# Three edits in an attention and MLP kernel: where the first loads are issued, which banks the first transposes use, and the order of the first layer's products

## The chip, the cores and the metric

The kernel runs on one core of one Trainium2 chip. A core has TensorE (PE, matmuls and transposes, results in PSUM banks), VectorE (DVE), ScalarE (ACT, table functions and copies), GpSimd (POOL) and SyncE (SP, which here only issues transfers). Each engine works through its own list of instructions in order and waits on semaphores for the others. Transfers between memory and the core run on 16 DMA engines; SP and ACT issue them to hardware queues (q1 is SP's, q10 ACT's in the profile), POOL to a software queue (q0).

The metric is device time in microseconds: the median of several runs. Before the change it is 442.35 us, from three runs between 442.12 and 442.97.

## What is computed

Eight batches of 12 heads, 448 positions, head size 64; then a two-layer MLP over the 3,584 rows:

```python
def rmsnorm(x, g):
    rms = np.sqrt(np.mean(x * x, axis=-1, keepdims=True) + 1e-06)
    return x / rms * g
q_n, k_n = (rmsnorm(q, g_q), rmsnorm(k, g_k))
scores = scale * np.matmul(q_n, k_n.transpose(0, 1, 3, 2))
scores = scores - np.max(scores, axis=-1, keepdims=True)
attn = np.exp(scores)
attn = attn / (np.sum(attn, axis=-1, keepdims=True) + 1e-09)
x = np.matmul(attn, v)                      # heads side by side: 3584 x 768
h = x @ w_in                                # 768 x 2048
g = gelu_tanh(h)
return g @ w_out                            # 2048 x 768
```

## The kernel before, in words

**Tiling.** A batch's positions stand on 112 partitions, four positions to each. Heads go in pairs (six pairs, `hp`), and in three chunks of four heads (two pairs) for loading. A pair fills 128 partitions once transposed. The first layer's 2,048 columns go in 16 blocks of 128 (`f`), over six steps of 128 inputs, one per pair (`c`); step `c` needs only that pair's x.

**A batch's way.** For each chunk q and k are loaded (`load`, L95), squared (L120 on ACT, L122 on POOL), summed over the head size (DVE, L127), turned into 1/rms by a logarithm and an exponential (ACT, L136 `lg` and L139 `rinv`), and multiplied (`nrmq`, `nrmk`, L149, on DVE or POOL). A pair is then transposed by PE (`trans`, L166, four transposes for q and four for k into the PSUM tile `tp`) and copied out, q to `qT` (L172 on ACT for the first pair, L174 on DVE for others), k to `kT` (L175, DVE) times `gcol`, the product of the two gain rows g_q and g_k. Scores (PE, L204) go through the exponential (ACT, L208). Sums and products with V (PE, L234) end in three DVE steps, `st`, `rc`, `rb` (L244 to L246), and in `xT` (L251).

**Order.** The schedule is written out by hand: each engine's order is the order of the calls. The first batch has an attention of its own (`first_attention`, L397), since nothing else is there to fill PE. Here `idle` (L144) multiplies zeros to keep PE at work. POOL squares and norms most of the first batch, and issues V's loads (L111), both halves of `win` (L483) and of `wout` (L489) between. `gpsimd_waits` (L529, `mark`) is a copy of one element that holds POOL until the second pair's `nrmk` is there.

**The start.** Before the first square, SP's list holds the first chunk's loads in halves of two heads (q, k, q, k), then the second chunk's the same way (q, k, q, k), then whole chunks. ACT's list begins with the loads of g_q and g_k (L68) and a table load (L437). POOL's begins with a memset of `ident`, a memset of `kT` (L84) and a select that finishes `ident`; its next instruction squares the second chunk's first half of q, and its next issues V's first two heads. A transfer takes one of eight hardware semaphores in turn (software transfers have their own), and the ninth waits until the first has landed. On DVE the order is: sums, `gcol` (L499), `gdiag` (L501), the first pair's `nrmq` and `nrmk`, three steps of `shift`, `kT`. PE multiplies by `gdiag` (L503, for `shift`), runs three fill products, the first pair's eight transposes, three more fill products, and the first scores. `ps_m` is a pool of two PSUM tiles that take turns.

**The end of the first batch's attention.** `first_attention` ends with the last pair's sums and products, and with two calls of `mm1_pair` (L331): each fills two blocks `f`, 12 products, into one PSUM tile `hh` of two banks, and has ACT take both through the gelu (L344). The main program then has DVE sum the next batch's squares, ACT load the exponential's table (L580), compute `lg` and `rinv`, load the gelu's table again (L581), and goes on with pairs 2 to 7.

Of the kernel before, what the change touches and what calls it, by code (L numbers as in the profile page):

```python
# [9 lines left out]
BF16 = mybir.dt.bfloat16  # L10
# [6 lines left out]
def kernel(  # L17
# [11 lines left out]
    nc = tc.nc  # L29
    B, H, S, D = q.shape  # L30
# [34 lines left out]
    nc.vector.memset(zeros, 0.0)  # L65
    grow = consts.tile([D, 2], F32)
    for i, row in enumerate((g_q, g_k)):
        nc.scalar.dma_start(grow[:, i:i + 1], row.rearrange("(d o) -> d o", o=1))  # L68
    EXP_SET, GELU_SET = "natural_log_exp_and_others", "gelu_apprx_tanh_and_others"

    gcol = consts.tile([128, 1], F32)
# [17 lines left out]
    def load(b, c, n, parts=1, eng=nc.sync):  # L89
        t = rawqk.tile([P, CH, NK, D], F32, tag=f"raw{n}", name=f"raw{n}")  # L90
        src = {"q": q, "k": k}[n]
        raws[n, b, c] = t
        m = CH // parts
        return [
            lambda i=i: eng.dma_start(  # L95
                t[:, i * m:(i + 1) * m],
                src[b, c * CH + i * m:c * CH + (i + 1) * m].rearrange(
                    "h (p t) d -> p h t d", t=NK
                ),
            )  # L100
            for i in range(parts)
        ]
# [49 lines left out]
            rinvs[b][:, c, "qk".index(n), 2 * j:2 * j + 2].to_broadcast([P, 2, NK, D]),  # L152
        )

    def trans(b, hp, home=None):

        c, j = hp // (CH // 2), hp % (CH // 2)
        if hp == 0:
            qT[b] = qkp.tile([128, HP, S], BF16, tag="qT", name="qT")
        if home is ps_m:  # L160
            tp = ps_m.tile([128, 2, 512], BF16, tag="mm", name="tp")
        else:
            tp = ps_s.tile([128, 2, 1024], BF16, tag="sc", name="tp")
        for i, n in enumerate("qk"):
            for t in range(NK):
                nc.tensor.transpose(  # L166
                    tp[:, i, t * P:(t + 1) * P],
                    nrms[n, b, c][:, j, t].rearrange("p a d -> p (a d)"),
                    ident[:P, :P],
                )  # L170
        if b == 0 and hp == 0:
            nc.scalar.copy(qT[b][:, hp], tp[:, 0, :S])  # L172
        else:
            nc.vector.tensor_copy(qT[b][:, hp], tp[:, 0, :S])  # L174
        nc.vector.tensor_scalar(  # L175
            kT[:, hp, :, :P], tp[:, 1, :S].rearrange("p (t s) -> p t s", s=P), gcol[:, 0:1],
            None, op0=ALU.mult,
        )

# [151 lines left out]
    def mm1_pair(i, cs=range(HP)):  # L331

        if cs[0] == 0:
            hs1[i] = ps_s.tile([128, 2, 512], F32, tag="sc", name="hh")
        h = hs1[i]
        for j in range(2):
            f = 2 * i + j
            for c in cs:
                nc.tensor.matmul(  # L339
                    h[:, j, :S], win[:, c, f * 128:(f + 1) * 128], xT[0][:, c],  # L340
                    start=(c == 0), stop=(c == HP - 1),
                )
        if cs[-1] == HP - 1:
            nc.scalar.activation(  # L344
                g[:, 2 * i:2 * i + 2, :S], h[:, :, :S], AF.Gelu_apprx_tanh
            )
# [50 lines left out]
    def first_attention(side, mid, early, late):  # L397


        warm = {}  # L400
        for i in range(HP * 2):
            for fn in side.get(i, ()):
                fn()
            scores(0, i // 2, 2 * (i % 2))
            for fn in mid.get(i, ()):
                fn()
            scores(0, i // 2, 2 * (i % 2) + 1)
            if i < 2:
                warm[i] = ps_o.tile([128, S], F32, tag=f"o{i}", name=f"o{i}")
                idle((6, 2)[i], warm[i])  # L410
            for fn in early.get(i, ()):
                fn()
            if i == 1:
                idle(4, warm[i])
            if i >= 2:
                pair_sums(0, i // 2 - 1, i % 2, waits=i < 6)
            for fn in late.get(i, ()):
                fn()
        nc.scalar.preload_act_table_set(GELU_SET)
        square(1, 2, "k", nc.scalar)  # L420
        for what in range(2):
            pair_sums(0, HP - 1, what)
        for i in range(2):
            mm1_pair(i)

    def plan(*entries):
        steps = {}
# [2 lines left out]
        return steps  # L430


    qh, kh = load(0, 0, "q", 2), load(0, 0, "k", 2)
    for i in range(2):
        qh[i]()
        kh[i]()
# [76 lines left out]
        shift, shift, -(D ** 0.5) * (1 + 2.0 ** -8), 60.0, op0=ALU.mult, op1=ALU.add  # L513
    )
    nc.vector.tensor_scalar(shift, shift, 0.0, None, op0=ALU.min)
    trans(0, 0, ps_m)
    idle(3, ps_m.tile([128, 512], F32, tag="mm", name="w")[:, :S])
    square(0, 0, "k", nc.scalar, slice(2, 4))
    totals0(1)
# [28 lines left out]
            (11, lambda: square(1, 1, "k", nc.gpsimd), lambda: square(1, 2, "q", nc.gpsimd),  # L548
             lambda: w_out_part(0), lambda: load_v(1, 0, CH), lambda: w_out_part(1))]
    mid = [(0, lambda: rsqrt0(1))] + [(2 * hp - 3, lambda hp=hp: rsqrt0(hp)) for hp in range(3, HP)]  # L550
    early = [(2 * hp + 1, lambda hp=hp: trans(0, hp + 1, ps_m)) for hp in range(HP - 1)]
    late = [(9, lambda: total(1, 0, "q"))]
    first_attention(plan(*side), plan(*mid), plan(*early), plan(*late))
    def normed1(c):
        for j in range(CH // 2):
            for n in "qk":
                normed(1, c, n, j, nc.vector)

    def transposed(b, c):
        for n in "qk":  # L560
            dma_trans(b, c, n)
# [12 lines left out]
    for b in range(B):  # L574
        m1, side = [], []
        if b == 0:

            m1 = [(1, lambda: total(1, 0, "k"), lambda: total(1, 1, "q"),
                   lambda: total(1, 1, "k"), lambda: total(1, 2, "k"), lambda: total(1, 2, "q"),
                   lambda: nc.scalar.preload_act_table_set(EXP_SET), lambda: rsqrt(1),  # L580
                   lambda: nc.scalar.preload_act_table_set(GELU_SET),  # L581
                   lambda: load_v(1, CH, 2 * CH), lambda: normed1(0), lambda: normed1(1)),
                  (3, lambda: loads(2, 0)),
                  (4, lambda: trans(1, 0, ps_m), lambda: normed1(2), lambda: transposed(1, 1),
                   lambda: loads(2, 1)),
                  (5, lambda: trans(1, 1, ps_m), lambda: loads(2, 2),
                   lambda: pool_waits(1, 2, "k", 1), lambda: square(2, 0, "q", nc.gpsimd),
                   lambda: square(2, 0, "k", nc.gpsimd)),
                  (6, lambda: trans(1, 4, ps_m)), (7, lambda: trans(1, 5, ps_m))]
            side += [(0, lambda: total(2, 0, "q"), lambda: total(2, 0, "k")),  # L590
                     (2, lambda: gain(1, 1))]

            for c, slots in ((1, (5, 7)), (2, (9, 10))):
                for n, slot in zip("qk", slots):
                    side += [(2 * c - 1, lambda c=c, n=n: square(2, c, n, nc.gpsimd)),
                             (slot, lambda c=c, n=n: total(2, c, n))]
        elif b + 1 < B:
            if b > 1:

                m1.append((0, lambda: gpsimd_waits(ess[b, HP - 1][:1, 0, 0, :1])))  # L600
            for c in range(NCH):
                m1 += [(0, lambda c=c: normed_all(b + 1, c)),
                       (4 * c + 4, lambda c=c: transposed(b + 1, c))]
            m1 += [(9, lambda: gain(b + 1, 0)), (14, lambda: gain(b + 1, 1))]
            side.append((3, lambda: gain(b + 1, 2)))
        if 0 < b and b + 2 < B:
            m1 += [(4, lambda: loads(b + 2, 1)), (8, lambda: loads(b + 2, 2))]
            for c, at in ((0, 1), (1, 9)):
                for i, (n, half) in enumerate((n, half) for n in "qk" for half in range(2)):
                    m1.append((at + i, lambda c=c, n=n, half=half: squared(b + 2, c, n, half)))  # L610
                m1 += [(at + 2, lambda c=c: total(b + 2, c, "q")),
                       (at + 4, lambda c=c: total(b + 2, c, "k"))]
            for n in "qk":
                m1.append((13, lambda n=n: square(b + 2, 2, n, nc.gpsimd)))
                side.append((0, lambda n=n: total(b + 2, 2, n)))
        m1 = plan(*m1)
        for f in range(nf // 2 if b == 0 else nf):
            if b > 0:
                mm1(b, f)
            elif f > 1:  # L620
                mm1_pair(f)
            for fn in m1.get(f, ()):
                fn()
        m2 += m2_parts(b)
        if b + 1 == B:
            for fn in m2:
                fn()
            break
        nc.scalar.preload_act_table_set(EXP_SET)
        if b + 2 < B:  # L630
            side += [(11, lambda: rsqrt(b + 2)),
                     (0 if b else 2, lambda: load_v(b + 2, 0, H))]
            if b + 3 < B:
                side.append((1, lambda: loads(b + 3, 0)))
        attention(b + 1, m2, 96 if b == 0 else 112, plan(*side))
# [30 lines left out]
```

## Time and profile before

| What | us |
|---|---|
| median of three runs | 442.35 |
| the profiled execution, its time | 442.38 |
| its span, first to last instruction | 440.6 |
| PE busy | 428.7 |
| ACT busy | 306.2 |
| first exponential (L208) starts | 9.78 |
| first product with V (L234) starts | 18.48 |
| first product of the first layer (L339) starts | 37.08 |
| from here PE has work without a gap worth naming | 47.86 |

An engine's busy time is no bound by itself: PE's 428.7 us hold fill products too. In the chain of waits a step starts when the step before it released it. The rows of the timeline give start, length, engine, line and operation, and in brackets how long the engine stood idle before and for whom.

### The profile page before, as it was taken

The page shows a single profiled execution, that of the slowest core. Times are in us where ns is not written, and L with a number is a line of the kernel's source. Part 1 is how long each engine was busy: PE and PEld are TensorE (multiplying, and loading weights), DVE is VectorE, ACT ScalarE, POOL GpSimd, SP SyncE. Part 2 cuts the span into 40 slices and gives each one's busy share as a digit, 9 for nine tenths or more (in the row PEclk, how much of TensorE's full clock was granted, in tenths as well). Part 3 has the DMA queues.
Part 4 walks back from the last instruction along what each step waited for, and adds up shares of the span by engine and source line. Part 5 has one row for each costly group of instructions (what it writes and reads, how often), then busy time and mean ns, then how long its engine had stood idle before and what let it go on. Part 6 is the DMA issues. An engine that isn't in the chain of part 4 may idle for free.

```text
span 440.6 us, 7132 instructions
## 1 busy us (share of the span) xinstructions
PE 428.7 (97%) x2827; PEld 215.2 (49%) x2827; DVE 258.9 (59%) x446; ACT 306.2 (69%) x407; POOL 149.9 (34%) x138
## 2 busy tenths in 40 slices
PE   8898999999999999999999999999999999999996
PEld 3344554455445554455445544455544554455563
DVE  5889846834688357763688536872588603881010
ACT  5896568946886688857888578856889348863310
POOL 5998126482202940065400950037400730000000
PEclk9999999999999999999999999999999999999999
DMA  8999999569801868139911779119831431111022
GB/s 202 241 233 238 211 190 259 80 152 250 169 18 55 190 111 176 36 93 224 194 37 36 170 159 182 37 37 230 128 70 36 99 65 37 38 36 37 0 72 72
DMA packets 79218, 54.02 MB, mean 123 GB/s; under 512 B 37456, under 2 KB 74192, under 8 KB 79184
## 3 DMA queue, kind: packets, MB, share of 16 engines
q1 hardware_dynamic: 62240, 41.66, 40.5%
q0 software_dynamic: 16624, 11.80, 18.2%
q8 instruction: 22, 0.36, 0.3%
q10 hardware_dynamic: 320, 0.10, 0.1%
q14 instruction: 12, 0.10, 0.1%
HBM read 45.61 MB, written 11.01 MB: 129 GB/s over the span
## 4 chain that ended last, share of the span: by engine, by line
PE 87%; ACT 8%; DMA 3%; DVE 1%; issue 0%; SPq 0%; POOL 0%; ACTq 0%; DVEq 0%
PE o L293 34%; PE h L272 29%; PE o L234 11%; PE sc L204 10%; ACT ex L208 6%; PE hh L339 3%; DMA vb<-in_v_dram 2%; DMA rawq<-in_q_dram 1%; ACT g L344 1%; PE tp L166 0%; SPq L95 0%; ACT L581 0%; ACT L580 0%; POOL g L122 0%; DVE st L244 0%
## 5 line engine op out<-in xcount | busy, mean ns | idle before, releaser
L208 ACT ACTIVATE ex<-sc,shift 112x896 bf16<-112x896 f32 x192 | 182.4, 1003 | 21.6 <-PE sc L204 21.2
L293 PE MATMUL o<-wout,g 128*128 128x384 bf16 (+1 forms) x956 | 161.2, 328 | 0.0
L272 PE MATMUL h<-xT,win 128*128 128x448 bf16 x672 | 128.3, 352 | 0.0
L293 PEld LDWEIGHTS <-g 128*128 128x128 bf16 (+1 forms) x956 | 81.4, 99 | 70.3 <-issue 23.4
L276 ACT ACTIVATE g<-h 128x448 bf16<-128x448 f32 x112 | 61.0, 544 | 75.2 <-PE h L272 72.3
L272 PEld LDWEIGHTS <-win 128*128 128x128 bf16 x672 | 65.8, 98 | 61.0
L127 DVE TENSOR_REDUCE ss<-sq 112x16 f32<-112x1024 f32 (+1 forms) x44 | 50.1, 1143 | 62.1 <-ACT sq L120 58.9
L204 PE MATMUL sc<-qT,kT 64*128 64x448 bf16 x384 | 58.8, 355 | 4.9 <-ACT ex L208 2.7
L317 DVE COPY osb<-o 128x384 f32<-128x384 f32 x51 | 28.1, 551 | 50.9 <-PE o L293 50.0
L220 DVE TENSOR_TENSOR es<-ex 112x896 bf16<-112x896 bf16 x72 | 43.9, 617 | 10.2 <-ACT ex L208 10.0
L529 POOL COPY mark<-es 1x1 bf16<-1x1 bf16 x5 | 0.9, 178 | 140.0 <-DVE es L222 140.0
L244 DVE STREAM_TRANSPOSE st<-o 128x448 f32<-128x448 f32 x48 | 31.2, 649 | 26.7 <-PE o L234 26.0
L234 PE MATMUL o<-ex,vb 112*64 112x448 bf16 x384 | 44.7, 354 | 0.6 <-DMA vb<-in_v_dram 0.6
L149 POOL TENSOR_TENSOR nrmk<-rawk,rinv 112x512 bf16<-112x512 f32 x40 | 44.5, 1130 | 0.0
L149 POOL TENSOR_TENSOR nrmq<-rawq,rinv 112x512 bf16<-112x512 f32 x40 | 41.0, 1043 | 4.8 <-ACT rinv L139 4.8
L204 PEld LDWEIGHTS <-kT 64*128 64x128 bf16 x384 | 17.2, 93 | 46.4 <-issue 41.2
L251 DVE TENSOR_TENSOR xT<-o,rb 128x448 bf16<-128x448 f32 x48 | 30.0, 625 | 3.8 <-PE o L234 1.7
L246 DVE STREAM_TRANSPOSE rb<-rc 128x448 f32<-128x448 f32 x48 | 31.0, 645 | 1.6
L122 POOL TENSOR_TENSOR sq<-rawq 112x1024 f32<-112x1024 f32 x9 | 17.1, 1894 | 40.1 <-DMA rawq<-in_q_dram 26.0
L234 PEld LDWEIGHTS <-vb 112*64 112x64 bf16 x384 | 20.9, 109 | 14.7 <-issue 2.3
L122 POOL TENSOR_TENSOR sq<-rawk 112x1024 f32<-112x1024 f32 (+1 forms) x11 | 19.5, 1774 | 4.9 <-DVE ss L127 3.3
L339 PE MATMUL hh<-xT,win 128*128 128x448 bf16 x96 | 19.1, 352 | 1.4 <-ACT g L344 0.8
(60 smaller groups left out, 235.9 us busy)
## 6 DMA issues: line engine op xcount, KB each, us to landing
rawq<-in_q_dram SPq DMA_DIRECT2D x22, 448.0 KB, 5.4
rawk<-in_k_dram SPq DMA_DIRECT2D x22, 448.0 KB, 6.5
vb<-in_v_dram POOLq DMA_DIRECT2D x6, 672.0 KB, 7.4
win<-in_moe_w_in_dram POOLq DMA_DIRECT2D x2, 1536.0 KB, 18.5
wout<-in_moe_w_out_dram POOLq DMA_DIRECT2D x2, 1536.0 KB, 21.6
out_dram<-osb SPq DMA_DIRECT2D x7, 336.0 KB, 2.7
out_dram<-osb SPq DMA_DIRECT2D x8, 288.0 KB, 2.7
out_dram<-osb SPq DMA_DIRECT2D x8, 240.0 KB, 2.7
```

Of the source, the lines that this page charges most:

```text
L122: eng.tensor_mul(sq, raw, raw)
L127: nc.vector.reduce_sum(sss[b][:, c, "qk".index(n), hs], sqs[n, b, c][:, hs], axis=AX.X)
L149: eng.tensor_mul(nrms[n, b, c][:, j].rearrange("p t a d -> p a t d"), raws[n, b, c][:, 2 * j:2 * j + 2], rinvs[b][:, c, "qk".index(n), 2 * ...
L204: nc.tensor.matmul(sc[:, a, :S], kT[r, hp, kt], qT[b][r, hp], start=True, stop=True,)
L208: nc.scalar.activation(exs[b, hp][:, kt], sc[:P, :, :S], AF.Exp, scale=scale, bias=shift)
L220: nc.vector.tensor_add(es[:, i], ex[:, 2 * i], ex[:, 2 * i + 1])
L234: nc.tensor.matmul(o[a * D:(a + 1) * D], vb[b % 2][:, 2 * hp + a, i] if what else ones, e[:, i, a], start=(i == 0), stop=(i == n - 1),)
L244: nc.vector.transpose(st.rearrange("p a b -> p (a b)"), oas[0])
L272: nc.tensor.matmul(h[:, :S], win[:, c, f * 128:(f + 1) * 128], xT[b][:, c], start=(c == 0), stop=(c == HP - 1),)
L276: nc.scalar.activation(g[:, f, (b % 2) * S:(b % 2 + 1) * S], h[:, :S], AF.Gelu_apprx_tanh)
L293: nc.tensor.matmul(o[j * m:(j + 1) * m, :HD], g[:, f, i * 128 + j * m:i * 128 + (j + 1) * m], wout[:, f, half * HD:(half + 1) * HD], start ...
L339: nc.tensor.matmul(h[:, j, :S], win[:, c, f * 128:(f + 1) * 128], xT[0][:, c], start=(c == 0), stop=(c == HP - 1),)
```

## The change

Four things change in the program. The loads of g_q and g_k are issued by POOL instead of ACT. The first chunk's two halves of k are issued by ACT instead of SP. The first pair's transposes go into two tiles of `ps_m`, q's into one and k's into the other; all other pairs keep one tile (the argument that chose the pool goes, each call had the same). Of the first 12 products of the first layer, the ten that need pairs 0 to 4 alone come first, five for each block, then the two that need the last pair; before, block 0 was finished before block 1 was begun.

```diff
     for i, row in enumerate((g_q, g_k)):
-        nc.scalar.dma_start(grow[:, i:i + 1], row.rearrange("(d o) -> d o", o=1))
+        nc.gpsimd.dma_start(grow[:, i:i + 1], row.rearrange("(d o) -> d o", o=1))
...
-    def trans(b, hp, home=None):
+    def trans(b, hp):
...
-        if home is ps_m:
-            tp = ps_m.tile([128, 2, 512], BF16, tag="mm", name="tp")
-        else:
-            tp = ps_s.tile([128, 2, 1024], BF16, tag="sc", name="tp")
+        first = b == 0 and hp == 0
+        tp = ps_m.tile([128, 2, 512], BF16, tag="mm", name="tp")
+
+        tps = tp, ps_m.tile([128, 2, 512], BF16, tag="mm", name="tp") if first else tp
         for i, n in enumerate("qk"):
             for t in range(NK):
                 nc.tensor.transpose(
-                    tp[:, i, t * P:(t + 1) * P],
+                    tps[i][:, i, t * P:(t + 1) * P],
...
-        if b == 0 and hp == 0:
+        if first:
             nc.scalar.copy(qT[b][:, hp], tp[:, 0, :S])
...
-            kT[:, hp, :, :P], tp[:, 1, :S].rearrange("p (t s) -> p t s", s=P), gcol[:, 0:1],
+            kT[:, hp, :, :P], tps[1][:, 1, :S].rearrange("p (t s) -> p t s", s=P), gcol[:, 0:1],
...
-        for i in range(2):
-            mm1_pair(i)
+
+        mm1_pair(0, range(HP - 1))
+        mm1_pair(0, [HP - 1])
+        mm1_pair(1)
...
-    qh, kh = load(0, 0, "q", 2), load(0, 0, "k", 2)
+    qh, kh = load(0, 0, "q", 2), load(0, 0, "k", 2, nc.scalar)
...
-    trans(0, 0, ps_m)
+    trans(0, 0)
```

How the lists of the engines move. SP's begins q, q (first chunk), then q, k, q, k (second), with the third chunk's first load waiting for the first k. ACT's begins with k's two halves, then the table load. POOL's begins: memset of `ident`, load of g_q, select of `ident`, load of g_k, memset of `kT`, and then as before. On PE the number and order of kinds of instructions stay; the second tile makes the first three fill products after the transposes wait for ACT's copy of `qT`, since they take the tile that it reads. `kT`'s copy on DVE waits for PE and for POOL's memset, and no longer for ACT.

More of the change, by code (lines that the diff above doesn't have):

```diff
@@ L550 @@
     mid = [(0, lambda: rsqrt0(1))] + [(2 * hp - 3, lambda hp=hp: rsqrt0(hp)) for hp in range(3, HP)]
-    early = [(2 * hp + 1, lambda hp=hp: trans(0, hp + 1, ps_m)) for hp in range(HP - 1)]
+    early = [(2 * hp + 1, lambda hp=hp: trans(0, hp + 1)) for hp in range(HP - 1)]
     late = [(9, lambda: total(1, 0, "q"))]
@@ L583 @@
                   (3, lambda: loads(2, 0)),
-                  (4, lambda: trans(1, 0, ps_m), lambda: normed1(2), lambda: transposed(1, 1),
+                  (4, lambda: trans(1, 0), lambda: normed1(2), lambda: transposed(1, 1),
                    lambda: loads(2, 1)),
-                  (5, lambda: trans(1, 1, ps_m), lambda: loads(2, 2),
+                  (5, lambda: trans(1, 1), lambda: loads(2, 2),
                    lambda: pool_waits(1, 2, "k", 1), lambda: square(2, 0, "q", nc.gpsimd),
                    lambda: square(2, 0, "k", nc.gpsimd)),
-                  (6, lambda: trans(1, 4, ps_m)), (7, lambda: trans(1, 5, ps_m))]
+                  (6, lambda: trans(1, 4)), (7, lambda: trans(1, 5))]
             side += [(0, lambda: total(2, 0, "q"), lambda: total(2, 0, "k")),
```

## The prediction

> **What bounds the kernel now.** I read the page first, then the chain of waits in order of time, then the timeline of the first 10 us and of 34 to 48 us, last the DMA queues slice by slice. The page says that PE sets the time, and where it does not:
>
> ```profile
> PE 428.7 (97%) x2827; PEld 215.2 (49%) x2827; DVE 258.9 (59%) x446; ACT 306.2 (69%) x407; POOL 149.9 (34%) x138
> PE 87%; ACT 8%; DMA 3%; DVE 1%; issue 0%; SPq 0%; POOL 0%; ACTq 0%; DVEq 0%
> ```
>
> From 47.86 us on the chain is PE work with ACT's exponentials between; nothing there is edited, so it moves as a block. What the change can move lies in two stretches of the chain (start, length, what):
>
> ```profile
> 2.75 5.91 DMA rawq<-in_q_dram
> 8.73 0.98 POOL g L122
> 9.71 8.73 DMA vb<-in_v_dram
> 18.48 0.95 PE o L234 x8
> ...
> 38.14 0.64 DVE xT L251
> 38.81 3.77 PE hh L339 x19
> 42.66 0.92 ACT g L344
> 43.60 1.28 ACT L580
> 45.60 1.28 ACT L581
> ```
>
> First, a half load of q lands, GpSimd squares it, then issues V's first load, and PE waits 0.61 us for that. Second, after the last pair's x, PE does 19 products before ACT can read the second pair. Beside the first chain runs another (start, length, engine, line; the bracket is idle time and its releaser):
>
> ```profile
> 6.04 0.34 DVE L499 TENSOR_TENSOR gcol<-grow 64x1 f32<-64x1 f32 x2
> 6.41 0.23 DVE L501 TENSOR_SCALAR gdiag<-ident,gcol 64x64 bf16<-64x64 bf16 x1
> 6.56 0.68 DVE L149 TENSOR_TENSOR nrmq<-rawq,rinv 112x512 bf16<-112x512 f32 x1
> 8.31 0.53 ACT L172 COPY qT<-tp 128x448 bf16<-128x448 bf16 x1 [0.90 <-PE tp L166]
> 8.87 0.45 DVE L175 TENSOR_SCALAR kT<-tp,gcol 128x448 bf16<-128x448 bf16 x1 [0.52 <-ACT qT L172]
> 9.38 0.55 PE L204 MATMUL sc<-qT,kT 64*128 64x448 bf16 x4 [0.54 <-ACT sq L120]
> 9.78 1.01 ACT L208 ACTIVATE ex<-sc,shift 112x896 bf16<-112x896 f32 x1 [0.42 <-PE sc L204]
> 13.08 0.18 POOL L529 COPY mark<-nrmk 1x1 bf16<-1x1 bf16 x1
> ```
>
> The reader should see that gcol, the product of the two gain rows, stands on DVE's queue ahead of the first norm, and that the two copies out of the first transposes run one after the other. From the mark on POOL works without a gap worth naming until 38.58, and pair 3's and 4's transposes at 22.2 and 26.3 us start within 0.15 us of its norms. So a late mark is late everywhere behind it; at the mark there is 0.28 us of slack (second nrmk ends 12.78, POOL comes free at 13.08).
>
> **Part 1: k's first halves on ACT's queue, q's on SP's.** SP issued one load each half microsecond (0.74, 1.19, 1.68, 2.18, 2.75). k's first half is now issued at 0.74 instead of 1.19, q's first load of the second chunk at about 1.68 instead of 2.75. The loads move at 237 packets a us when full (783 in 3.3 us), a half load is 224 and 16 for its semaphore. The bytes ahead of each load are the same, so k can gain between 0 and 0.45 us, while q's first half, now sharing with k's, can lose as much. lg needs both squares: I take 0, with -0.4 to +0.4. For the half that GpSimd waits for, bounds -1.07 and 0, taken -0.2. ACT's own queue issues two loads where it issued two gain rows (0.55 and 0.61 us), so its table load stays at 1.96.
>
> **Part 2: the gain rows on GpSimd's queue.** This part is not in the words of the change and costs most by my count. The first row is issued after the ident memset (ends 0.94); GpSimd's issues take 0.72 to 1.2 us, then comes the 0.29 us select, so the second row goes out at about 2.05 and kT's memset (2.66) ends near 5.5, still ahead of all that reads it. When does the second row land? Now:
>
> ```profile
> grow<-in_g_q_dram ACTq DMA_DIRECT2D x1, 0.2 KB, 3.0
> grow<-in_g_k_dram ACTq DMA_DIRECT2D x1, 0.2 KB, 4.6
> vb<-in_v_dram POOLq DMA_DIRECT2D x1, 112.0 KB, 8.7
> ```
>
> From ACT, issued at 1.32, it landed at 5.94, just ahead of gcol. From GpSimd the trace has one load at the start, V's, and it was slow: issued at 9.71, the software queue moves no packet before 15.9 us, though at 162.31, with the other queues empty, the same kind of load moves its first 1.7 us after issue. By 9.71 SP had issued 16 half loads' worth, 3,584 packets and 192 for semaphores; 3,444 were moved by 15.9. V began when some 330 of what had been issued before it were left, as if it stood in one line with them. For the second gain row: it is ready at 2.05 + 1.7 = 3.75. The loads from SP and ACT move their first packet some 1.0 us after issue (0.74, and none is moved before 1.75), so those issued by 2.7 are ahead, six half loads (1,440); less 330 makes 1,110, which the trace reaches at 6.4 us (seven: 7.2). Its 64 packets of 4 bytes took 0.6 us for the one row and 1.8 for the other in the trace, take 1.0, and 0.65 from last packet to landing (5.3 to 5.94): 8.05, and 8.85 with seven. I take 8.0. Below: it takes its turn at once, 3.75 + 1.3 (ACT's 3.0 less 1.7) = 5.05, no delay. Above: as slow as V's, 2.05 + 8.7 = 10.75.
>
> At 8.0 gcol is 2.05 us late. Behind it on DVE wait gdiag, both norms, the shift, kT; for these PE's transposes, ACT's copy and first exponential.
>
> **Part 3: two banks.** qT's copy waits for q's four transposes (end 7.95) instead of all eight (8.27): it starts 0.32 us earlier. kT no longer waits for it and starts at about 8.37 instead of 8.87. But the three fill products behind the transposes now write the bank that qT's copy reads, so they wait for its end (8.52), and PE's scores are queued behind them: three at 0.187 us make 9.12 instead of 9.38. Gain 0.26 us, bounds 0 and 0.5 (kT's own).
>
> Parts 1 to 3: the first exponential moves by 2.05 - 0.26 = +1.79. The mark moves by 1.79 - 0.28 = +1.5. PE and ACT get 0.6 back at V's wait, then meet POOL's norms, late by 1.5, at 22.2: sum +1.4. With 5.05 it is -0.3 (the smaller of part 1's and part 3's), with 8.85 +2.3, with 10.75 +4.2.
>
> **Part 4: products without the last x in front.** Ten instead of five run from 37.08, ten at 0.187 us, to 38.95; x is there at 38.77. Then 14 instead of 19 remain: 14 x 0.187 + 0.2 gives 41.8 instead of 42.6, and ACT's second gelu ends at 42.7 instead of 43.58, its table load at 44.0 instead of 44.88. But lg also waits for DVE's five sums, which end at 44.39 and do not move. lg goes from 44.90 to 44.41: gain 0.49, not 0.88. PE waits for that ACT chain at 47.86 and is full after it, so it lasts. Bounds: 0 (a wait unseen) and 0.88.
>
> **Sum.** +1.4 - 0.5 = +0.9 us. The profiled execution took 442.38 (span 440.6 and 1.8 around it), 0.03 over the median: 443.3. Against the median, 0.2% is 0.9 us, about what a measurement of this kernel can tell from no change.
>
> **Rivals.**
> A, not slower: GpSimd's queue takes its turn among the others, the second row lands by 5.94, gcol stays. It decides at that landing: 0.54 us past 5.94 (part 3 and the mark's slack) the start alone breaks even, 1.0 us past it the whole change. For it: from 16 us on both queues move alike (264 and 261 packets in 15.9 to 17.5). Against it: the 6.2 us before V's first packet. Time: 442.38 - 0.3 - 0.5 = 441.6.
> [...]
> B: the row waits as long as V's load did, landing at 10.75: +4.2 - 0.5 = 446.1. For it: it is also the first load of that queue, should a first load be slow in itself. Against: far less is in line.
> C, nothing comes of it: the row lands near 7.0, and the 0.5 us that the start then loses cancel part 4: 442.4. For it: the wait for V, which ends at 18.44 by the loads ahead of it, hides up to 0.6 us from PE. Against: not from POOL.
>
> **Chances.** The forecast 0.50, with its own range 442.5 to 444.6 (part 2 at 7.5 to 8.85, part 4 at 0.2 to 0.9); A 0.28 (441.0 to 442.0); B 0.08; C 0.14. Faster by over 0.2% (under 441.5) is some two thirds of A and little else: 0.22. Slower by over 0.2% (over 443.2) is B and two thirds of the forecast: 0.41. The rest, 0.37, is within 0.2%. The range 441.2 to 444.9 leaves out B and the ends.
>
> **What would show it.** In the changed profile: the second gain row's time to landing (5.9 us from 2.05 by the forecast, under 4 by A); gcol's start (8.0, or 6.0) and an idle DVE before it; qT's copy starting before the last transpose, kT's not waiting for ACT; the fill products idle until that copy ends; the mark at 14.6 with POOL idle ahead of it; no wait for V at PE; lg 0.5 us earlier against x of the last pair, released by DVE's sums. I am wrong if gcol starts before 7, or if V's load moves with the gain rows ahead of it in its queue.

## The result, and the profile after

The changed kernel takes 445.96 us (median of six runs, 445.28 to 446.62); the kernel before, run beside it on the same chip, 442.21 (six runs, 441.82 to 442.97). The ratio is 1.0081, 95% interval [1.0066, 1.0096]: slower by 0.8%. The forecast was 443.3 with a range to 444.9, so the direction was the one forecast and the time lies above the range. The profiled execution took 445.28, with a span of 443.5 us against 440.6.

The page of the changed kernel, its busy times and the share of each engine in the chain of waits: PE's busy time grows by 1.6 us although it does the same 2,827 matmuls, and DMA, which had 3% of the chain through q's half load and V's, has 1%.

```profile
PE 430.3 (97%) x2827; PEld 216.0 (49%) x2827; DVE 258.8 (58%) x446; ACT 306.0 (69%) x407; POOL 152.0 (34%) x140
...
PE 86%; ACT 7%; POOL 2%; DVE 2%; DMA 1%; issue 1%; POOLq 0%; DVEq 0%; ACTq 0%
```

The chain of waits of the changed kernel's first 20 us (start, length, what) says where that 1% is. Before, the chain went through q's half load, GpSimd's square and V's load. Now it goes through the second gain row, `gcol`, and then mostly through PE:

```profile
2.34 5.97 DMA grow<-in_g_k_dram
...
8.42 0.15 DVE gcol L502
...
9.33 1.24 PE w L144 x3
10.57 0.39 PE tp L166 x4
...
11.56 1.28 PE w L144 x3
12.84 0.86 PE sc L204 x4
```

The timeline of the same stretch, and in its last line the step that part 4 is about (start, length, engine, line; in brackets idle time and its releaser):

```profile
1.16 5.09 PE L144 MATMUL w<-zeros 128*128 128x448 bf16 x16 [1.16 <-DVE zeros L65]
1.32 0.69 POOL L68 DMA_DIRECT2D grow<-in_g_q_dram  x1 [0.38 <-issue]
...
2.34 0.56 POOL L68 DMA_DIRECT2D grow<-in_g_k_dram  x1
...
6.53 0.31 ACT L136 ACTIVATE lg<-ss,eps 112x16 f32<-112x16 f32 x1 [0.83 <-DVE ss L127]
...
8.42 0.34 DVE L502 TENSOR_TENSOR gcol<-grow 64x1 f32<-64x1 f32 x2 [1.92 <-DMA grow<-in_g_k_dram]
...
8.94 0.68 DVE L149 TENSOR_TENSOR nrmq<-rawq,rinv 112x512 bf16<-112x512 f32 x1
...
9.12 0.21 PE L506 MATMUL gall<-gdiag,rows 64*112 64x64 bf16 x1 [2.87 <-DVE gdiag L504]
9.26 1.30 PE L144 MATMUL w<-zeros 128*128 128x448 bf16 x3
...
10.98 0.53 ACT L172 COPY qT<-tp 128x448 bf16<-128x448 bf16 x1 [3.37 <-PE tp L166]
...
11.42 0.45 DVE L175 TENSOR_SCALAR kT<-tp,gcol 128x448 bf16<-128x448 bf16 x1 [0.69 <-PE tp L166]
...
13.37 1.01 ACT L208 ACTIVATE ex<-sc,shift 112x896 bf16<-112x896 f32 x1 [1.33 <-PE sc L204]
...
16.21 0.18 POOL L532 COPY mark<-nrmk 1x1 bf16<-1x1 bf16 x1 [3.61 <-DVE nrmk L149]
...
47.66 0.38 ACT L136 ACTIVATE lg<-ss,eps 112x96 f32<-112x96 f32 x1 [0.32 <-DVE ss L127]
```

The fill products of the kernel before, for comparison:

```profile
1.16 5.75 PE L144 MATMUL w<-zeros 128*128 128x448 bf16 x16 [1.16 <-DVE zeros L65]
...
7.01 0.74 PE L144 MATMUL w<-zeros 128*128 128x448 bf16 x3
```

The reader should see two delays, one behind the other. `gcol` starts at 8.42 instead of 6.04 and all of DVE's list with it. And PE, whose fill products are used up at 6.25, stands idle for 2.87 us; after that three fill products take 1.30 us, where three took 0.74 before. The windows of the same kernel (start and end, PE's busy time and instructions, granted clock, DMA) name the reason:

```profile
5.00:8.00 3.00, 1.25 (x7) 1.00 0.97 245
8.00:9.00 1.00, 0.00 (x0) 0.73 1.12 290
9.00:15.00 6.00, 5.63 (x23) 0.50 1.14 241
15.00:16.00 1.00, 1.00 (x7) 0.86 1.24 257
```

The granted clock is 1.00, then 0.50 from 8.45 to 15.28 us (6.83 us), then 1.00 again. In the kernel before it stays at 1.00 through the start.

A part of the 2.87 us of idle time is not the row's doing. The first 16 fill products are the same in both kernels, but end at 6.91 in the kernel before and at 6.25 here. In both they start 0.37 us apart at first and 0.19 later, though the view reads 1.00 throughout; when the faster stretch begins differs from one execution to the next (the 16 products end at 5.72 in e4's profile below, at 7.12 in e7's).

**From the start to the end.** The timelines of all kernels run here have one thing in common, and it makes the rest easy to read. Times in us, from the profiled execution of each (e1 to e12 are the experiments below; e6 and e10 have further waits between the mark and the last `xT` and are left out):

| Kernel | `gcol` | first exponential | mark | last pair's `xT` | `lg` of the next batch | span |
|---|---|---|---|---|---|---|
| before | 6.04 | 9.78 | 13.08 | 38.14 | 44.90 | 440.6 |
| after | 8.42 | 13.37 | 16.21 | 41.37 | 47.66 | 443.5 |
| e5 more fill | 8.40 | 11.80 | 14.64 | 39.65 | 45.95 | 441.8 |
| e1 rows only | 7.70 | 12.13 | 14.97 | 39.99 | 46.75 | 442.6 |
| e2 rows back | 8.08 | 14.71 | 17.55 | 42.58 | 48.87 | 444.6 |
| e3 k's halves only | 8.22 | 14.64 | 17.48 | 42.52 | 49.28 | 445.0 |
| e9 rows first | 10.14 | 15.81 | 18.65 | 43.69 | 49.98 | 445.6 |
| e12 no rows | 6.39 | 10.61 | 13.45 | 38.47 | 44.76 | 440.5 |
| e4 order only | 6.67 | 10.41 | 13.29 | 38.32 | 44.61 | 440.3 |
| e7 banks and order | 6.42 | 9.93 | 13.02 | 38.05 | 44.34 | 440.0 |
| e8 banks only | 6.38 | 9.78 | 13.29 | 38.33 | 45.09 | 440.8 |
| e11 | 7.93 | 9.78 | 12.76 | 37.78 | 44.07 | 441.0 |

From the mark to the last `xT` it is 25.0 to 25.2 us in every row. From there to `lg` it is 6.76 with the old order of products and 6.29 with the new one. From `lg` to the end it is 395.6 to 395.9, in all rows but e11's. So what a kernel does to the start is settled at the mark, and the new order is worth 0.47 wherever it is used.

### The profile page after: what moved, and what is told of

It is laid out like the page before. It is cut to its first block, busy times and chain, and to the rows that moved or that the text cites. A ratio compares the mean times of both kernels' runs of the same rounds, so it can differ in the third digit from the quotient of the medians.

```text
span 443.5 us, 7133 instructions
## 1 busy us (share of the span) xinstructions
PE 430.3 (97%) x2827; PEld 216.0 (49%) x2827; DVE 258.8 (58%) x446; ACT 306.0 (69%) x407; POOL 152.0 (34%) x140
## 3 DMA queue, kind: packets, MB, share of 16 engines
q0 software_dynamic: 16688, 11.80, 18.7%
## 4 chain that ended last, share of the span: by engine, by line
PE 86%; ACT 7%; POOL 2%; DVE 2%; DMA 1%; issue 1%; POOLq 0%; DVEq 0%; ACTq 0%
PE o L293 33%; PE h L272 29%; PE o L234 11%; PE sc L204 10%; ACT ex L208 6%; PE hh L339 2%; DMA grow<-in_g_k_dram 1%; DVE ss L127 1%; PE w L144 1%; PE tp L166 1%; PE o L144 1%; POOL nrmq L149 0%; POOL nrmk L149 0%; ACT g L344 0%; ACT L584 0%
## 5 line engine op out<-in xcount | busy, mean ns | idle before, releaser
L293 PEld LDWEIGHTS <-g 128*128 128x128 bf16 (+1 forms) x956 | 81.4, 99 | 70.3 <-issue 23.4
```

The costliest lines, as they stand in the source:

```text
L293: nc.tensor.matmul(o[j * m:(j + 1) * m, :HD], g[:, f, i * 128 + j * m:i * 128 + (j + 1) * m], wout[:, f, half * HD:(half + 1) * HD], start ...
```

## The experiments

Three theories were set against each other. Theory 1: the late second gain row costs, directly and through PE's idle time, which halves its clock. Theory 2: k's halves on ACT's queue make the first squares late. Theory 3: fill products that wait for `qT`'s copy starve PE. Ratios are to the kernel before, run on the same chip beside each.

**More fill products (e5).** The changed kernel with 28 instead of 16 fill products ahead of the gains' product, and nothing else:

```diff
-    idle(16, ps_m.tile([128, 512], F32, tag="mm", name="w")[:, :S])
+    idle(28, ps_m.tile([128, 512], F32, tag="mm", name="w")[:, :S])
```

> The changed kernel with 28 instead of 16 fill products at the start, 2.2 us more work for PE, which ends near 8.8 at full clock and so covers most of the wait for gcol. Nothing else moves. If the halved clock of PE is a part of the loss (theory 1), the granted clock stays at 1.0, the first exponential comes near 12 instead of 13.4, and the time falls from 446 to some 444.3 us. If the clock does not matter, since ACT and GpSimd set the pace there, 445.9.

Measured: 443.75 (443.45 to 445.34, eight runs), ratio 1.0036 [1.0022, 1.0050]. Its timeline, and its windows over the stretch shown above:

```profile
9.06 0.19 PE L506 MATMUL gall<-gdiag,rows 64*112 64x64 bf16 x1 [1.06 <-DVE gdiag L504]
9.18 0.74 PE L144 MATMUL w<-zeros 128*128 128x448 bf16 x3
```

```profile
8.00:9.00 1.00, 0.00 (x0) 1.00 1.11 284
9.00:15.00 6.00, 4.98 (x34) 1.00 1.15 253
```

`gcol` is as late as in the changed kernel (8.40), but the clock stays at 1.00, three fill products take 0.74 us, and the first exponential comes at 11.80 instead of 13.37. The halved clock is therefore worth 1.57 us at the mark, 1.7 of the span, 2.2 between the medians. What is left over the kernel before, 1.2 us of span and 1.6 of the median, is the late row and the rest of the change. One of the eight executions took 445.34 with a mean granted clock of 0.996, where the others have 0.998 to 1.000: it seems that the fill does not always keep the clock up.

**Loads held back (e6).** The changed kernel, where SP's loads of the second and third chunk wait until DVE has done the first sums (a memset behind them writes into their tile). The rows are issued at 1.32 and 2.34 as before.

```diff
+    nc.vector.memset(raws["q", 0, 1][:1, 0, 0, :1], 0.0)
+    for i in range(2):
+        qh1[i]()
+        kh1[i]()
+    loads(0, 2)
```

> The changed kernel with SP's loads of the second and third chunks held back until DVE has summed the first pair (a one-element memset of the tile that they overwrite stands behind the sums), so that four half loads and not seven are issued ahead of the second gain row. If GpSimd's row stands in line behind the loads issued before it, it lands by 6.8 instead of 8.3. If GpSimd's first loads are slow in themselves, it lands near 8.3 all the same. The time is not the point; the second chunk's loads come some 4 us later and it may be slower.

The DMA issues of the changed kernel and then of this one (size and us from issue to landing):

```profile
grow<-in_g_q_dram POOLq DMA_DIRECT2D x1, 0.2 KB, 5.4
grow<-in_g_k_dram POOLq DMA_DIRECT2D x1, 0.2 KB, 6.0
```

```profile
grow<-in_g_q_dram POOLq DMA_DIRECT2D x1, 0.2 KB, 4.8
grow<-in_g_k_dram POOLq DMA_DIRECT2D x1, 0.2 KB, 3.9
```

And the start of DVE's step in this one's timeline:

```profile
6.34 0.34 DVE L501 TENSOR_TENSOR gcol<-grow 64x1 f32<-64x1 f32 x2
```

Same queue, same issue time: the second row lands 2.1 us sooner when less is being loaded, `gcol` waits for nothing and the first exponential is back at 9.74. Were GpSimd's first loads slow in themselves, the second row would have landed as before. In the changed kernel none of its packets starts before 6.25 us, when SP's and ACT's queues have started 1,191; here none starts before 5.05, when those queues have started 927 of the 960 packets of the four half loads. The time (445.73, a single run) says nothing about the row, since the held loads make other work late (PE waits 0.94 us for V at 19.43, and its clock is halved from 20.0 to 23.4).

**The rows by other queues (e1, e2, e3).** e1 is the kernel before with the rows on GpSimd's queue alone; e2 the changed kernel with the rows on ACT's queue behind k's halves; e3 the kernel before with k's halves on ACT's queue and the rows behind them. The first diff is e1's, the second what e2 and e3 have in common (the old place of the rows goes).

```diff
-        nc.scalar.dma_start(grow[:, i:i + 1], row.rearrange("(d o) -> d o", o=1))
+        nc.gpsimd.dma_start(grow[:, i:i + 1], row.rearrange("(d o) -> d o", o=1))
```

```diff
     qh, kh = load(0, 0, "q", 2), load(0, 0, "k", 2, nc.scalar)
     for i in range(2):
         qh[i]()
         kh[i]()
+    for i, row in enumerate((g_q, g_k)):
+        nc.scalar.dma_start(grow[:, i:i + 1], row.rearrange("(d o) -> d o", o=1))
```

> The kernel before with the gain rows alone moved to GpSimd's queue. Theory 1 (the late second row costs the time, a part of it by PE standing idle until its granted clock halves): the row lands near 8, gcol starts 2 us or more later than 6.04, the granted clock shows 0.5 for some microseconds after 8, and the time is 445.5 to 447 us, since the gain of the product order (0.5) is missing. Theory 2 (k's halves on ACT's queue make the first squares late): 442.2 as before. Theory 3 (the fill products that wait for ACT's copy starve PE): 442.2.

> The changed kernel with the gain rows back on ACT's queue, behind k's two halves; k's halves, two banks and product order stay. Theory 1: the loss goes, 441.5 to 442.5 us, clock 1.0 throughout; the rows may land near 6.5, some tenths later than before. Theory 2: 444 to 446, the first logarithm stays late (6.5 against 5.94) and the first exponential with it. Theory 3: 444 to 446.

> The kernel before with k's first halves on ACT's queue, the gain rows behind them there. Theory 2: slower by 1 us or more. Theory 1: 442.0 to 442.9, the first logarithm at 6.5 instead of 5.94 as in the changed kernel, gcol where the rows let it, the loss hidden in part by the wait for V.

| Run | second row issued | landed after | median | ratio |
|---|---|---|---|---|
| e1 | 2.34 | 5.3 | 444.43 (5 runs) | 1.0039 [1.0024, 1.0054] |
| e2 | 2.29 | 5.7 | 446.55 (4 runs) | 1.0087 [1.0070, 1.0104] |
| e3 | 2.28 | 5.8 | 445.85 (4 runs) | 1.0079 [1.0064, 1.0095] |

All three miss the times that theory 1 gave them: e1 is faster than its 445.5 to 447, e2 and e3 are slower than their 441.5 to 442.5 and 442.0 to 442.9. By the times alone e2 and e3 came out as theory 2 said. The profiles tell the two apart: in e2 and e3 `lg` starts at 6.44 and 6.37, and `gcol` waits for the second row until 8.08 and 8.22. From ACT's queue a row issued at 2.3 lands as late as from GpSimd's (5.7 and 5.8 us after its issue, against 5.3 in e1 and 6.0 in the changed kernel). So it isn't the software queue that makes the row late; it is that it is issued at 2.3, when several half loads are on their way. Moving the rows alone costs about half of the whole change, with the clock halved for 3.41 us (from 8.29) instead of 6.83.

The executions of one kernel show the price of the clock once more. A stretch of 3.41 us at half clock takes 0.004 off the mean granted clock of an execution. e1's executions took 444.29 to 444.70 at 0.995 or 0.996, and 443.54 at 0.999; e2's 446.37 to 446.95 at 0.991 or 0.992, and 445.42 at 0.996; e3's 445.56 to 445.93 at 0.996, and 446.84 (the profiled one) at 0.992. So one such stretch goes with some 1 us. e2 and e3 have one cost more, which their timeline shows (e3):

```profile
8.22 2.00 DVE L499 TENSOR_TENSOR gcol<-grow 64x1 f32<-64x1 f32 x2 [1.89 <-DMA grow<-in_g_k_dram]
8.96 1.05 POOL L120 TENSOR_TENSOR g<-rawk 112x512 f32<-112x512 f32 x1
...
10.40 0.68 DVE L147 TENSOR_TENSOR nrmq<-rawq,rinv 112x512 bf16<-112x512 f32 x1
```

Two products of 64 elements that take 0.34 us elsewhere take 2.00 here, and end at 10.22, just behind POOL's square (10.01). In e2 `gdiag` takes 1.66 instead of 0.23 in the same way. Once late, DVE's small steps meet POOL's squares here (the one at 8.96 in e3, at 9.31 in e2).

**The rows in front of k's halves (e9).** The changed kernel with the rows on ACT's queue ahead of k's halves:

```diff
-        nc.gpsimd.dma_start(grow[:, i:i + 1], row.rearrange("(d o) -> d o", o=1))
+        nc.scalar.dma_start(grow[:, i:i + 1], row.rearrange("(d o) -> d o", o=1))
```

> The changed kernel with the gain rows issued by ACT ahead of k's halves instead of by GpSimd, so that only they move up in the line. Theory 1 (the late second row costs, through gcol, the norms and the clock that falls while PE idles): the second row lands near 6, gcol starts at 6.0 to 6.7 with at most 0.8 us of waiting, PE idles under 2.1 us ahead of the gains' matmul, no clock drop before 16 us, first exponential near 9.8, mark near 13.1, time 441.5 to 442.9. Theory 2 (k's halves on ACT's queue make the first squares late): k's halves are issued even later here (about 2.0 and 2.5), so the first exponential stays at 12 or later, whether gcol is early or not, and the time is 444 or more.

Measured: 447.38 (446.96 to 447.82, four runs), ratio 1.0117 [1.0104, 1.0130], the slowest of all. Theory 1's time is missed by 4.5 us; what theory 2 says happens:

```profile
1.32 0.61 ACTq L68 DMA_DIRECT2D grow<-in_g_k_dram  x1
...
8.87 0.63 ACT L120 ACTIVATE sq<-rawk 112x512 f32<-112x512 f32 x1 [3.84 <-DMA rawk<-in_k_dram]
...
10.14 0.33 DVE L502 TENSOR_TENSOR gcol<-grow 64x1 f32<-64x1 f32 x2
```

`gcol` no longer waits for the row, which landed 5.6 us after its issue. But k's first half, issued at about 2.0 instead of 0.74, is there only at 8.8, and k's sum, `lg` and the norms wait for it. PE idles for 5.23 us and its clock is halved for 6.83. What ACT issues at 2.0 to 2.3, a row (e2, e3) or a half load (here), lands 5.7 to 6.9 us later: the two have only changed places.

**No rows at all (e12).** The changed kernel with both gain rows filled with ones by DVE; the gains are left out of the result.

```diff
-    for i, row in enumerate((g_q, g_k)):
-        nc.gpsimd.dma_start(grow[:, i:i + 1], row.rearrange("(d o) -> d o", o=1))
+    nc.vector.memset(grow, 1.0)
```

> The changed kernel without the load of the gain rows: DVE fills the two rows with ones instead (the gains are left out of the result), so no row is late, no packet of it is ahead of k's halves, and k's halves still stand at the head of ACT's queue. It measures what the new home of k's halves costs by itself. Theory 1 (the row's landing is the cost, k's halves are not): first squares as in the changed kernel, 4.5 and 5.1, lg near 6.5, norms from 6.9, PE idle under 1.5 us, no clock drop before 16 us, first exponential 9.9 to 10.3, time 441.6 to 442.8, that of banks and order alone. Theory 2 (k's halves on that queue cost as much as in the run with rows in front of them, where k's first square came at 8.87): k's square at 6 or later, first exponential 11 or later, time 443.5 or more.

Measured: 442.19 (441.87 to 442.61, eleven runs), ratio 0.9998 [0.9989, 1.0007].

```profile
5.06 0.61 ACT L119 ACTIVATE sq<-rawk 112x512 f32<-112x512 f32 x1
6.50 0.31 ACT L135 ACTIVATE lg<-ss,eps 112x16 f32<-112x16 f32 x1 [0.83 <-DVE ss L126]
...
7.70 1.53 DVE L148 TENSOR_TENSOR nrmk<-rawk,rinv 112x512 bf16<-112x512 f32 x1
...
10.61 1.01 ACT L207 ACTIVATE ex<-sc,shift 112x896 bf16<-112x896 f32 x1 [1.30 <-PE sc L203]
...
13.45 0.18 POOL L531 COPY mark<-nrmk 1x1 bf16<-1x1 bf16 x1 [1.46 <-DVE nrmk L148]
```

Without the load of the rows the whole loss is gone. The expectation for the first exponential (9.9 to 10.3) is missed by 0.3 us, because the second norm takes 1.53 us beside POOL's square instead of 0.68. k's halves at the head of ACT's queue do have a price in this profile: first squares 0.5 to 0.9 us later, `lg` 0.56, mark 0.37. In the span the new order, 0.47, pays for it. A single profile doesn't settle the size: in e7 below, with k's halves on SP's queue as before, `lg` starts at 6.54 too.

**`gcol` behind the norms (e10, e11).** e10 is the changed kernel with `gcol` and `gdiag` moved on DVE behind both norms, and the gains' product on PE behind the transposes. e11 is the same in the kernel before, with the two banks and the new order and all loads as before; it was meant to be faster than both kernels.

```diff
+    def gains():
+        for a in range(2):
+            nc.vector.tensor_mul(gcol[a * D:(a + 1) * D], grow[:, 0:1], grow[:, 1:2])
+        nc.vector.tensor_scalar(gdiag, ident[:D, :D], gcol[:D, 0:1], None, op0=ALU.mult)
+        nc.tensor.matmul(gall[:P, :D], rows, gdiag, start=True, stop=True)
...
-    trans(0, 0)
+    trans(0, 0, gains)
```

> The changed kernel with nothing altered in its loads: only the product gcol and gdiag are moved on DVE's queue behind both norms, the gains' matmul behind the transposes, the shift behind kT's copy. Theory 1: the second row still lands near 8.3, but the norms start near 6.6 and the transposes near 7.3, PE idles under 2 us, no clock drop, first exponential 9.9 to 10.4, mark near 13.2 to 13.6, time 441.7 to 443.0. If the delay came from the transfers or the squares themselves and not through gcol's place in DVE's queue, the norms start at 8 or later all the same and the time is 445 or more.

> The kernel before with the two banks, the order of the products and gcol behind the norms (rows on ACT in front and all other loads as before). Theory 1: DVE never waits for the row, first exponential 9.5 to 9.9, x of the last pair near 38.1, lg near 44.3, time 441.4 to 442.3, 0 to 0.9 below before. If what stands behind gcol does not bound the start at all, it equals the run with banks and order alone, 442.3.

Measured: e10 444.80 (443.96 to 444.97, five runs), ratio 1.0056 [1.0044, 1.0068], so 1.2 us better than the changed kernel but 1.8 above what was expected. The norms no longer wait for the row; they start at 7.24, behind an `lg` at 6.65, where 6.6 was expected. Then three steps of DVE are stretched beside POOL's work, and `kT`, which needs `gcol` as well, is late:

```profile
7.85 1.53 DVE L149 TENSOR_TENSOR nrmk<-rawk,rinv 112x512 bf16<-112x512 f32 x1
9.30 1.47 DVE L507 TENSOR_TENSOR gcol<-grow 64x1 f32<-64x1 f32 x2
...
10.96 0.44 DVE L177 TENSOR_SCALAR kT<-tp,gcol 128x448 bf16<-128x448 bf16 x1
...
12.49 1.01 ACT L210 ACTIVATE ex<-sc,shift 112x896 bf16<-112x896 f32 x1 [3.03 <-PE sc L206]
```

And the clock, which was expected to stay up, is halved from 12.34 to 15.75. The one execution with a mean clock of 1.000 took 443.96, the others, at 0.994 to 0.996, 444.78 to 444.97. `gcol`'s place ahead of the norms is thus part of the delay, not all of it.

e11 took 442.20 (441.73 to 446.62, twelve runs) against 442.17, ratio 1.0015 [0.9995, 1.0035]: no gain to be told from nothing. Its profile (an execution of 442.79) has the mark 0.32 us and `lg` 0.83 us earlier than before, and loses more than that later, at the second batch's V, issued by GpSimd at 41.27. First the timeline of e11, then the same step in the kernel with banks and order alone (e7), and the DMA issues of e7 from 38 to 46 us:

```profile
75.40 0.95 PE L237 MATMUL o<-ex,vb 112*64 112x448 bf16 x8 [1.04 <-DMA vb<-in_v_dram]
```

```profile
74.48 0.95 PE L235 MATMUL o<-ex,vb 112*64 112x448 bf16 x8
```

```profile
vb<-in_v_dram POOLq DMA_DIRECT2D x1, 448.0 KB, 32.9
```

In e7 that load was issued at 41.55 and landed 32.9 later, at 74.45, 0.03 us before PE's product with it. In the kernel before it landed at 74.3, for a product at 75.02. In e11 PE stood ready at 74.36, but the load landed only at 75.4, later than in e7 although issued 0.28 us sooner; in e4 and e12, issued at 41.82 and 41.96, it landed at 72.5 and 71.1. So a faster start comes close to this transfer, whose landing varies by more than the gain; why it does is not shown.

**Banks and order (e4, e7, e8).** The kernel before with the order (e4), the two banks (e8) or both (e7):

```diff
-        for i in range(2):
-            mm1_pair(i)
+        mm1_pair(0, range(HP - 1))
+        mm1_pair(0, [HP - 1])
+        mm1_pair(1)
...
+            tp2 = ps_m.tile([128, 2, 512], BF16, tag="mm", name="tp") if b == 0 and hp == 0 else tp
```

> The kernel before with the product order alone. By the prediction's working lg comes 0.49 us earlier, released by DVE's sums, and the time is 441.7 us. If that wait is hidden anyway: 442.2. If ACT's second gelu set it: 441.3.

> The kernel before with two banks and the product order, all loads as before. By the prediction's working the first exponential comes 0.26 us earlier, which GpSimd's norms and the wait for V hide, and the order gives 0.49: 441.7 us. If the 0.26 reaches the end too: 441.4. If the waiting fill products cost (theory 3): 442.2 or more.

> The kernel before with two banks for the first pair's transposes alone. First exponential 0.26 us earlier (9.5); time 442.1 to 442.2, as the mark on GpSimd's queue does not move (13.08) and the wait for V grows by as much. Theory 3: slower than before by 0.3 us or more.

Measured, twelve runs each: e4 442.13, ratio 1.0004 [0.9981, 1.0028]; e7 442.31, 1.0003 [0.9991, 1.0015]; e8 442.61, 1.0011 [1.0000, 1.0023]. No median moves by what can be told from no change, though the order's 0.47 us stand in every profile that has it (spans 440.3 and 440.0 for e4 and e7). Two of e4's executions took 446.25 and 446.75, at mean clocks of 0.996 and 0.994, and one of e11's 446.62 at 0.992; none of these was profiled. By the times alone theory 3 is not refuted at its own size: it gave 0.3 us or more for e8, which is 0.47 over the kernel before, and 442.2 or more for e7. The profiles speak against it: from `gcol` to the first exponential it is 3.40 us in e8, 3.51 in e7 and 3.40 in e5, against 3.74 before, although the fill products wait. PE isn't starved, and nothing of that size could carry the whole loss.

## Why the prediction was wrong, point by point

**What failed.** The sum of parts 1 to 3 carried the row's 2.05 us one for one to the first exponential: "2.05 - 0.26 = +1.79". Behind `gcol` the prediction named PE's transposes as waiting, and did not ask what PE does meanwhile. It has 16 fill products, which end at 6.91 in the profile before and ended at 6.25 here; with `gcol` at 8 it had to idle for some 2 us, and its granted clock was halved for 6.83 us, in which six fill products, the transposes and the scores took longer (three fill products 1.30 us instead of 0.74, four transposes 0.58 instead of 0.36, four scores 0.93 instead of 0.55). First exponential +3.59 us instead of +1.79; e5 takes away that term alone and has +2.02, and the mark at 14.64 where the prediction said 14.6. The missing term, which the sum put at nothing, is the 1.6 to 2.2 us that separate e5 from the changed kernel.

When the clock falls is only partly shown. The half-clock stretches last 3.41 us (e1, e6, e10) or 6.83 us (the changed kernel, e9). The clock fell 2.19 us after the last fill product here and 2.12 us after it in e1, and it did not fall in e4, where PE was idle for 1.60 us. Nor is it one gap that counts: in e10 the clock fell though no gap was longer than 1.49 us; the 3.41 us ahead of the fall hold 2.00 us of idle time in all. In e6 it fell after 3.41 us with only 1.46, so no threshold can be read from these runs.

**Part 2, the row.** Landing at 8.3, forecast 8.0; `gcol` +2.38 us, forecast +2.05; the range of 5.05 to 10.75 held it. The time from issue to landing, 6.0, is the forecast's 5.9. It was issued at 2.34 instead of 2.05, and that is most of the 0.3. The reason given, that the row lands after what was being loaded before it, is what e6, e2 and e3 show. The line is not a strict one: the row's packets began after 1,191 others, where 1,440 had been issued ahead of it. The heading was too narrow, though: it blamed GpSimd's queue, and ACT's is as slow for a row issued at 2.3 (5.7 us to landing in e2, 5.8 in e3).

**Part 1, k's halves.** Taken at 0, bounds -0.4 to +0.4. In the changed kernel `lg` came 0.59 us later than before, hidden behind `gcol`; in e12, where nothing hides it, 0.56 late at `lg`, 0.37 at the mark, nothing in the time (the order pays). Over all profiles `lg` starts at 5.82 to 6.54, 6.08 in the mean, with k's halves on SP's queue (six kernels), and at 6.33 to 6.65, 6.45 in the mean, with them at the head of ACT's (seven). So the value was not 0 but some 0.4, at the edge of its bounds. It also has a price that was not seen at all: with two queues issuing loads, the rows have more ahead of them (six half loads issued before 2.34 instead of four), 6.0 us to landing against 5.3 in e1.

**Part 3, two banks.** From the first norm to the first exponential it was 3.22 us before and is 2.87 in e5, where the clock is full: 0.35 gained, forecast 0.26. `kT` doesn't wait for ACT any more and the three fill products wait for the copy, both as predicted. In the changed kernel the halved clock covers all of it.

**Part 4, the order.** Forecast 0.49, measured 0.47 (6.29 against 6.76 from `xT` to `lg`), with `lg` released by DVE's sums as predicted.

**From the mark on.** "A late mark is late everywhere behind it" holds: 25.0 to 25.2 us to the last `xT` in every kernel of the table. The wait for V at 18.4 is gone, as predicted.

**The rivals.** A needed the row by 5.94; it landed at 8.3 and fell. That GpSimd's queue takes its turn among the others was the author's assumption, and no run shows it for these rows: 0.2 KB on a queue of their own took 4.5 to 6.0 us to land (e1 and the changed kernel). B's time, 446.1, is close to the measured one by luck: it needed a landing at 10.75. C, a row at 7.0 whose cost the order cancels, did not happen; e12 comes out even as well, but by another cost, that of k's halves.

## What to carry to other kernels

When a step is moved and something waits longer, ask of every engine behind it, PE above all, what it does during the wait: here its fill work ran out, the idle time was paid a second time in the clock (0.50 for 6.83 us), and a dozen more fill products were worth 1.7 us of the 2.9 that the span had grown by. A tiny load that everything needs is worth issuing before the big ones: the second gain row landed at 5.9 to 6.9 when ACT issued it at 1.32 or 1.33 (the kernel before, e4, e7, e8, e9), and at 7.6 to 8.3 when it was issued at 2.3, by either queue (e1, e2, e3, the changed kernel). What it overtakes became late in its place (e9: k's first half landed 6.9 us after its issue), so it helps to count the first issues as one budget for all queues. Before tuning a start, look for the next transfer that lands just in time (here V's at 74.3 to 75.4 us): it can take the gain back.

## What was not expected of the hardware

DVE's steps were stretched while POOL worked: a norm 1.53 us instead of 0.68 (e10, e12), two products of 64 elements 2.00 instead of 0.34 (e3), `gdiag` 1.66 instead of 0.23 (e2); the other way round a square of POOL's took 2.01 instead of 1.05 while DVE did its norms (the changed kernel). Which operations do this was not tried.

The six runs of the changed kernel fall into two groups, 445.28 to 445.49 and 446.42 to 446.62. The profiled one belongs to the first. A longer stretch at half clock doesn't explain them: another 3.41 us would take the mean granted clock from 0.991 to some 0.987, and the second group has 0.990, 0.990 and 0.992. No execution of the second group was profiled, and it stays open.

The second gain row's landing varies from one kernel to the next with the same loads ahead of it: `gcol` came at 6.04 in the profile of the kernel before, with no wait, and at 6.38 to 6.67 in e4 and e8, where it waited for the row. So the row was just in time from the beginning.
